# A state-space scan ahead of a SwiGLU layer: chunks of 64 tokens on two row tiles, y in four PSUM banks, one list of steps

## The chip, the cores and the metric

The kernel runs on one core of one Trainium2 chip. The metric is the device time of one execution in microseconds. The kernel before the change takes 417.41 us (median of three runs, 417.39 to 417.42); its profiled execution spans 414.9 us.

## What is computed

Two parts follow one another. The first is a Mamba-2 scan for 4 batches x 8 heads, 768 tokens, head size D = 32 and state size N = 16, all float32. The reference does it in chunks; the length of a chunk changes the amount of work, not the mathematical result:

```python
for c in range(nc):                                   # chunks of a sequence
    cum = np.cumsum(log_a[:, :, sl], axis=-1)
    L = np.exp(cum[..., :, None] - cum[..., None, :]) * causal
    y_intra = (einsum('bhin,bhjn->bhij', Cc, Bc) * L) @ xc
    y_inter = einsum('bhin,bhnd->bhid', Cc, state) * exp(cum)[..., None]
    y[:, :, sl] = y_intra + y_inter
    state = exp(sum(la)) * state + sum_j(Bc_j x_j exp(cum_last - cum_j))
```

The second part takes the 3072 x 256 result y, divides each token by its root mean square, multiplies by a gain, and does a gated layer with d_ff = 1536: `(silu(xn @ w_gate) * (xn @ w_val)) @ w_out`. The output is 3072 x 256, float32.

## The kernel before

Tokens are handled in six blocks of 512; a block has two pairs p of row tiles (128 tokens each), so there are twelve pairs. Block b's feed-forward products stand beside the scan of block b + 1. The gate, value and output products of all but part of the first block use a seven-product scheme on 2 x 2 blocks (`P`, `C`, `O` steps), with the sums done on VectorE.

A chunk is 128 tokens, that is one row tile. TensorE's array is used in tiles in the scan: `tile_position=(row, column)` says where a small matmul lies in the 128 x 128 array. The products C B^T for a pair (step `g`, four row tiles of 32 rows, one for each two heads):

```python
def product(p, todo):
    T = st[p]["T"]
    for i in range(2):
        for q, g in todo:
            r = slice(32 * q, 32 * q + 32)
            nc.tensor.matmul(out=g[:, 256 * i:256 * i + 256], lhsT=T[r, i, 0],
                             rhs=T[r, i, 1:3].rearrange("p t m -> p (t m)"),
                             start=(i == 0), stop=True, tile_position=(32 * q, 0), ...)
```

In the first two pairs this is called for two row tiles at a time (`products`), in the others for all four at once. VectorE then multiplies the products with the decays L, a tile of 128 x (2 x 8 x 128) (`decayed`, `decayed_one`). What a chunk adds to the state (step `A`) and the states (step `S`):

```python
for i in range(n):
    for q in range(NQ):
        nc.tensor.matmul(out=A_ps[32 * q:32 * q + 32, i], lhsT=s["Bd"][:, i, 2 * q:2 * q + 2],
                         rhs=s["x"][:, i, 2 * q:2 * q + 2], tile_position=(0, 32 * q), ...)
# states: one multiplication by a mask for the pair, then for each chunk
nc.vector.scalar_tensor_tensor(out=S, in0=state[g - 1], scalar=fcol[:, k:k + 1],
                               in1=new[:, i], op0=ALU.mult, op1=ALU.add)
```

The output of a pair (step `y`) goes to one pair of PSUM banks; `inter` uses the state, `intra` the chunk's own tokens:

```python
def inter(i, opens):                       # 32 x 64 tiles
    for q in range(NQ):
        nc.tensor.matmul(out=y[o:o + 64, q // 2, i * P:(i + 1) * P], lhsT=S[r],
                         rhs=CdT[r], tile_position=(32 * q, o), ...)
def intra(i, opens):                       # 128 x 32 tiles
    for h in range(NH):
        nc.tensor.matmul(out=y[o:o + 32, h // 4, i * P:(i + 1) * P], lhsT=s["x"][:, i, h],
                         rhs=Ls[p][:, i, h], tile_position=(0, o), ...)
if not first:
    inter(0, True)
intra(0, first)
intra(1, False)
inter(1, False)
```

ScalarE squares y (step `sq`) and copies it out (step `yt`, by VectorE in block 0), one instruction each. The decays of the first four pairs come by matmul: a mask of -2^100 (`mask`, two bf16 matmuls of 512 columns a half of the heads), then sums of logarithms (`sums`, eight matmuls of 128 columns and two of 512), then an exponential. Those of the other pairs are broadcast by DMA from a table of row sums in DRAM (`spread`), VectorE subtracts the token's sum (`sub`), ScalarE takes the exponential and GpSimd clears the part above the diagonal (`ex`).

PSUM has eight banks: three pairs (0, 1 and 2) in the first block, of which 0 and 1 later become four banks for the feed-forward products, and two single banks (`bank`), which serve all small results in turn, among them the two other banks of `g`.

The order of all instructions is written by hand, as a list of steps for each kind of block; each engine executes its own steps in the list's order.

Of the kernel before, what the change touches and what calls it, by code (L numbers as in the profile page):

```python
# [20 lines left out]
def kernel(  # L21
# [47 lines left out]
    NBLK = T // TB  # L69

# [61 lines left out]
    fetched = []  # L132

    def fetch(k=1):
        for _ in range(min(k, len(pieces))):
            n, c, w = pieces.pop(0)
            if n == "o":
                src, dst, shape = wsrc[n][:, c:c + w], wo[:, c:c + w], (w, DM)
            else:
# [8 lines left out]
            fetched.append((w16[:, :, :, 3], (w32[:, :, :, 0], w32[:, :, :, 1]), dst,  # L148
                            [P] + list(shape)))
# [33 lines left out]
    def weight(k):  # L183
        words16, (lo, hi), dst, shape = fetched[k]
        e, f = parts.pop((k, "e")), parts.pop((k, "f"))
        nc.vector.scalar_tensor_tensor(out=dst, in0=f, scalar=2.0 ** -20, in1=e,
                                       op0=ALU.mult, op1=ALU.mult)
        fetch()
# [3 lines left out]
    a_sb = const.tile([BH, S], FP32, name="a_sb")  # L192
# [4 lines left out]
    for p in range(2):  # L197
        load_x(p)
    fetch(2)
    gcol = const.tile([P, 2], FP32, name="gcol")  # L200
    nc.sync.dma_start(out=gcol, in_=moe_rms_g.rearrange("(t p) -> p t", p=P))
    fetch(4)
    load(2)
    load_x(2)
    fetch(3)
    load(3)
    load_x(3)
# [16 lines left out]
                            fill=0.0, base=-1, channel_multiplier=1)  # L224
    hmask = const.tile([P, NH], FP32, name="hmask")
# [21 lines left out]
    nc.vector.tensor_scalar_add(mid[0:64], mid[0:64], -1.0)  # L247
    ident16 = const.tile([P, P], BF16, name="ident16")
    nc.vector.tensor_copy(out=ident16, in_=ident)
    never16 = const.tile([P, P], BF16, name="never16")  # L250
    nc.vector.tensor_copy(out=never16, in_=never)
# [22 lines left out]
    early = nrm.tile([P, 3, NC, BH], FP32, tag="xn", name="early", bufs=1)  # L274
    la0, full, fsel = early[:, 0], early[:, 1], early[:, 2]
# [59 lines left out]
    fcol = const.tile([P, NC * NB], FP32, name="fcol")  # L335

    def chunk_sums():
        ps["c"] = full_ps = bank("full_ps", (P, NC, BH))
        nc.tensor.matmul(out=full_ps.rearrange("p c h -> p (c h)"), lhsT=ones, rhs=laf,
                         start=True, stop=True)  # L340

    def chunk_decays():
        nc.scalar.activation(out=full, in_=ps.pop("c"), func=AF.Exp)
        nc.gpsimd.tensor_tensor(
            out=fsel.rearrange("p c (b h) -> p (c b) h", h=NH),
            in0=full.rearrange("p c (b h) -> p (c b) h", h=NH),
            in1=hmask.unsqueeze(1).to_broadcast([P, NC * NB, NH]), op=ALU.mult)

    def chunk_column():
        nc.vector.reduce_sum(out=fcol, in_=fsel.rearrange("p c (b h) -> p (c b) h", h=NH),  # L350
                             axis=AX.X)


    Ls = {}

    def pair_tile(g):
        if g // 2 not in Ls:
            Ls[g // 2] = ssd.tile([P, 2, NH, P], FP32, tag="L", name="L", bufs=2)
        return Ls[g // 2][:, g % 2]

    def mask(e):
        for i in range(2):
            nc.tensor.matmul(out=e[:, i], lhsT=ident16,  # L363
                             rhs=never16.unsqueeze(1).to_broadcast([P, 4, P]),
                             start=True, stop=False, skip_group_check=True)

    def sums(todo):

        for p, half, e in todo:
            rows_of = [slice(32 * q, 32 * q + 32) for q in (2 * (p % 2), 2 * (p % 2) + 1)]  # L370
            row = rows[p // 2]
            for o in range(4):
                for i, r in enumerate(rows_of):
                    nc.tensor.matmul(out=e[:, i, o * P:(o + 1) * P],  # L374
                                     lhsT=sel[r, 4 * half + o:4 * half + o + 1].to_broadcast([32, P]),
                                     rhs=row[r, 0], start=False, stop=False,
                                     tile_position=(r.start, 0), skip_group_check=True)
            for i, r in enumerate(rows_of):
                nc.tensor.matmul(out=e[:, i], lhsT=row[r, 1],
                                 rhs=sel[r, 4 * half:4 * half + 4].unsqueeze(2).to_broadcast([32, 4, P]),  # L380
                                 start=False, stop=True, tile_position=(r.start, 0),
                                 skip_group_check=True)

    def decay(p, half, e):
        pair_tile(2 * p)
        nc.scalar.activation(
            out=Ls[p][:, :, 4 * half:4 * half + 4].rearrange("p i h m -> p i (h m)"),
            in_=e, func=AF.Exp)

    def spread(g):  # L390
        b, c = divmod(g, NC)
        o = (c * BH + b * NH) * P
        nc.sync.dma_start(out=pair_tile(g).rearrange("p h m -> p (h m)"),
                          in_=rowv[o:o + NH * P].partition_broadcast(P))

    def subtract(g):
# [3 lines left out]
            out=L, in0=L, in1=tok[:, c, b * NH:(b + 1) * NH].unsqueeze(2).to_broadcast([P, NH, P]),  # L400
            op=ALU.subtract)

    def exponential(g):
        L = pair_tile(g)
        nc.scalar.activation(out=L, in_=L, func=AF.Exp)
        nc.gpsimd.affine_select(out=L, in_=L, pattern=[[0, NH], [1, P]], compare_op=ALU.is_ge,
                                fill=0.0, base=0, channel_multiplier=-1)
# [50 lines left out]
    def products(p, half, g):  # L458

        ps["g", p, half] = g  # L460
        product(p, [(2 * half + k, g[:, k]) for k in range(2)])

    def product(p, todo):
        T = st[p]["T"]
        for i in range(2):
            for q, g in todo:
                r = slice(32 * q, 32 * q + 32)
                nc.tensor.matmul(  # L468
                    out=g[:, 256 * i:256 * i + 256], lhsT=T[r, i, 0],
                    rhs=T[r, i, 1:3].rearrange("p t m -> p (t m)"),  # L470
                    start=(i == 0), stop=True, tile_position=(32 * q, 0),
                    skip_group_check=True)

    def decayed(p, half):
# [3 lines left out]
        nc.vector.tensor_tensor(out=L, in0=g.rearrange("p q (i m) -> p q i m", i=2), in1=L,  # L478
                                op=ALU.mult)

    def products_at_once(p, g=None):

# [668 lines left out]
```

## Time and profile before

The profile counts busy time of each engine: TensorE's matmuls (PE), its weight loads (PEld, beside the matmuls), VectorE (DVE), ScalarE (ACT), GpSimd (POOL).

| what | value |
|---|---|
| time, median of three | 417.41 us |
| span of the profiled execution | 414.9 us |
| VectorE, busy | 304.4 us, 667 instructions |
| ScalarE, busy | 229.7 us, 462 instructions |
| data moved by DMA | 27.99 MB, 67 GB/s over the span |
| granted clock of TensorE | full throughout |

The page's chain that ended last is followed back from the last instruction, each step to what released it. Its shares by line tell where the time of the bounding engine goes: 28% and 21% are the gate and value products of line 732 and 23% the output products of line 822, while the scan's lines 468 (g), 550 and 541 (y) and 501 (A) have 4, 3, 2 and 1%. A line such as `L468 PE MATMUL g<-T 32*128 32x256 f32 x192` reads: line, engine, operation, result and operands, the weights' tile in the array, the moving operand's partitions x elements, number of records. Behind it stand the busy time, the mean of one in ns, and the engine's idle time before it. Since matmuls are pipelined, one record's duration is longer than the distance to the next.

### The profile page before, as it was taken

How to read it: one execution, taken by the hardware profiler on the slowest of the kernel's cores; microseconds unless marked ns; L12 is line 12 of the kernel's file. 1: busy time of each engine (PE TensorE's matmuls, PEld its weight loads, DVE VectorE, ACT ScalarE, POOL GpSimd, SP SyncE). 2: the span in 40 equal slices, each digit the busy share in tenths (PEclk: the TensorE clock that was granted, in tenths of full speed). 3: DMA queues.
4: the chain of work that ended last, by engine and by line, in shares of the span. 5: the costliest groups of instructions: out<-in, count | busy, mean ns of one | idle time of the engine just before them, and what ended most of it. 6: DMA issues, size and time to landing. Idle time of an engine off the chain costs nothing.

```text
span 414.9 us, 7936 instructions
## 1 busy us (share of the span) xinstructions
PE 409.7 (99%) x3100; PEld 343.6 (83%) x3100; DVE 304.4 (73%) x667; ACT 229.7 (55%) x462; POOL 39.0 (9%) x48
## 2 busy tenths in 40 slices
PE   7999999999999999999999999999999999999997
PEld 4575478888878799888899887899988889988897
DVE  6899998979679986376986477795575784556672
ACT  3998989877656316745428645526646521245410
POOL 3020000013000005000013100014100000000000
PEclk9999999999999999999999999999999999999999
DMA  9988849001007112703070503070100000100001
GB/s 113 232 200 157 256 102 368 21 0 52 1 2 152 44 61 42 112 2 101 11 145 25 77 2 101 2 154 1 52 2 0 2 2 1 52 0 2 0 2 51
DMA packets 86852, 27.99 MB, mean 67 GB/s; under 512 B 76032, under 2 KB 80640, under 8 KB 86816
## 3 DMA queue, kind: packets, MB, share of 16 engines
q1 hardware_dynamic: 82656, 27.24, 28.3%
q10 hardware_dynamic: 4160, 0.26, 0.8%
q8 instruction: 24, 0.39, 0.4%
q14 instruction: 12, 0.10, 0.1%
HBM read 24.22 MB, written 3.28 MB: 66 GB/s over the span
## 4 chain that ended last, share of the span: by engine, by line
PE 98%; DVE 1%; issue 0%; ACT 0%
PE gate L732 28%; PE o L822 23%; PE val L732 21%; PE o L764 5%; PE g L468 4%; PE gate L648 3%; PE y L550 3%; PE y L541 2%; PE tp L434 2%; PE gate L658 2%; PE A_ps L501 1%; PE e L363 1%; PE rb L613 1%; PE idle L266 1%; PE ms L591 1%; PE e L374 1%
## 5 line engine op out<-in xcount | busy, mean ns | idle before, releaser
L744 DVE TENSOR_TENSOR c<-val,p 128x512 f32<-128x512 f32 x99 | 67.4, 686 | 49.8 <-PE val L732 37.5
L738 ACT COPY p<-gate 128x512 f32<-128x512 f32 x99 | 57.8, 588 | 68.1 <-PE gate L732 62.6
L732 PE MATMUL gate<-tx,sw 128*128 128x256 f32 x264 | 65.0, 382 | 0.0
L732 PEld LDWEIGHTS gate<-tx,sw 128*128 128x128 f32 x264 | 48.7, 190 | 8.2 <-issue 2.0
L757 DVE TENSOR_TENSOR h<-c 128x256 f32<-128x256 f32 x99 | 41.0, 432 | 19.0 <-ACT c L753 19.0
L753 ACT ACTIVATE c<-c 128x256 f32<-128x256 f32 x99 | 38.2, 413 | 11.5 <-DVE c L744 10.7
L732 PE MATMUL val<-xn,sw 128*128 128x256 f32 x132 | 34.1, 383 | 0.0
L732 PE MATMUL val<-tx,sw 128*128 128x256 f32 x132 | 33.8, 384 | 0.0
L822 PE MATMUL o<-wo,h 128*128 128x128 f32 x240 | 33.7, 277 | 0.0
L732 PE MATMUL gate<-tx,wgv 128*128 128x256 f32 x132 | 33.1, 381 | 0.0
L732 PE MATMUL val<-xn,wgv 128*128 128x256 f32 x132 | 33.1, 379 | 0.0
L732 PE MATMUL gate<-xn,wgv 128*128 128x256 f32 x132 | 33.0, 380 | 0.0
L822 PE MATMUL o<-two,s 128*128 128x128 f32 x240 | 32.0, 275 | 0.0
L569 POOL TENSOR_TENSOR sq<-sq 128x256 f32<-128x256 f32 x12 | 10.1, 841 | 227.3 <-ACT sq L568 197.2
L822 PE MATMUL o<-two,h 128*128 128x128 f32 x240 | 30.9, 275 | 0.0
L822 PEld LDWEIGHTS o<-wo,h 128*128 128x128 f32 x240 | 29.9, 192 | 1.0 <-issue 0.6
L822 PEld LDWEIGHTS o<-two,s 128*128 128x128 f32 x240 | 29.9, 192 | 0.3
L838 ACT COPY v<-o 128x256 f32<-128x256 f32 x15 | 5.6, 372 | 43.6 <-PE o L822 43.6
L822 PEld LDWEIGHTS o<-two,h 128*128 128x128 f32 x240 | 28.9, 192 | 0.1
L732 PEld LDWEIGHTS val<-tx,sw 128*128 128x128 f32 x132 | 24.5, 190 | 4.6 <-DVE h L757 1.0
L732 PEld LDWEIGHTS val<-xn,sw 128*128 128x128 f32 x132 | 24.4, 190 | 4.2 <-issue 0.7
L732 PEld LDWEIGHTS gate<-tx,wgv 128*128 128x128 f32 x132 | 24.8, 190 | 3.5 <-issue 0.2
(159 smaller groups left out, 696.9 us busy)
## 6 DMA issues: line engine op xcount, KB each, us to landing
L<-rowd SPq DMA_DIRECT2D x16, 512.0 KB, 4.7
xr<-in_x_dram SPq DMA_DIRECT2D x24, 128.0 KB, 3.5
wr<-in_moe_w_out_dram SPq DMA_DIRECT2D x6, 512.0 KB, 7.2
wr<-in_moe_w_gate_dram SPq DMA_DIRECT2D x5, 512.0 KB, 6.3
wr<-in_moe_w_val_dram SPq DMA_DIRECT2D x5, 512.0 KB, 6.6
out_dram<-ob SPq DMA_DIRECT2D x9, 256.0 KB, 2.2
br<-in_B_dram SPq DMA_DIRECT2D x22, 64.0 KB, 4.2
cr<-in_C_dram SPq DMA_DIRECT2D x22, 64.0 KB, 3.0
```

What stands on the lines that cost most here:

```text
L434: nc.tensor.transpose(out=tp[:, k], in_=src[:, i].rearrange("p h n -> p (h n)"), identity=ident)
L468: nc.tensor.matmul(out=g[:, 256 * i:256 * i + 256], lhsT=T[r, i, 0], rhs=T[r, i, 1:3].rearrange("p t m -> p (t m)"), start=(i == 0), stop= ...
L550: nc.tensor.matmul(out=y[o:o + 32, h // 4, i * P:(i + 1) * P], lhsT=s["x"][:, i, h], rhs=Ls[p][:, i, h], start=opens, stop=True, tile_posi ...
L569: nc.gpsimd.tensor_tensor(out=sqs[blk][:, tk], in0=sq2[:, 0], in1=sq2[:, 1], op=ALU.add)
L648: nc.tensor.matmul(out=gv[:, k], lhsT=w[:, t, fs], rhs=xns[0][:, t], start=(t == 0), stop=(t == 1))
L732: nc.tensor.matmul(out=dst[:, half[w]], lhsT=lhsT, rhs=rhs, start=(k in (1, 2, 5) and w == 0), stop=True, skip_group_check=True)
L738: nc.scalar.copy(out=t, in_=Xs[j])
L744: nc.vector.tensor_tensor(out=t, in0=Zs[j], in1=a, op=ALU.add)
L753: nc.scalar.activation(out=u, in_=src[:, half[0]], func=AF.Silu)
L757: nc.vector.tensor_tensor(out=hidden_tile(blk, j)[:, c // 10 - 1, c % 10 - 1], in0=u, in1=src[:, half[1]], op=ALU.mult)
L764: nc.tensor.matmul(out=o, lhsT=hs_[blk, f // 2][:, f % 2, k // 2, (k % 2) * P:(k % 2 + 1) * P], rhs=wo[:, f], start=opens, stop=(f == NF - ...
L822: nc.tensor.matmul(out=o[t] if apart else o[:, t * P:(t + 1) * P], lhsT=lhsT[:, t], rhs=rhs, start=(k in (1, 2, 4, 5) and j == 0 and (apar ...
```

## The change

A chunk is now 64 tokens, half a row tile. Two chunks of the same row tile are handled at once: the second index u in `halves` picks tokens 0 to 63 or 64 to 127, which lie on the upper or lower half of the array's rows (in `A` and intra y) or go to the lower or upper half of its columns (in `g`). The decays L within a chunk have a quarter of the elements of a 128-token chunk, and there are twice as many chunks, so L is half as large. In return there are twice as many states. Matmuls are shorter and there are more of them, in up to eight tiles at a time. Different row tiles write to different PSUM banks: `A` takes both single banks, y the pair 2 and both single banks, four in all. All steps of all blocks stand in one list with the block's number ahead of each step, in a new order in which steps of neighbouring blocks mix; the list also says which pair of banks each step of the first block takes, and when each piece of the weights is fetched.

The core of the diff (cuts marked by [...]; setup of masks and constants, the table of row sums in DRAM and the list itself left out):

```diff
+    HC = P // 2
+    halves = [slice(0, HC), slice(HC, P)]
[...]
-            Ls[g // 2] = ssd.tile([P, 2, NH, P], FP32, tag="L", name="L", bufs=2)
+            Ls[g // 2] = ssd.tile([P, 2, NH, HC], FP32, tag="L", name="L", bufs=LBUFS)   # LBUFS = 4
[...]
+    def sums(p, e):                     # once a pair, was: once for each half of the heads
+        for h in range(NH):
             for i, r in enumerate(rows_of):
+                for u in halves:
+                    nc.tensor.matmul(out=e[u, i, h * HC:(h + 1) * HC],
+                                     lhsT=sel[r, h:h + 1].to_broadcast([32, HC]), rhs=row[r, 0, u],
+                                     tile_position=(r.start, u.start), ...)
+        for i, r in enumerate(rows_of):
+            for u in halves:
+                nc.tensor.matmul(out=e[u, i], lhsT=row[r, 1, u], rhs=sel[r]...([32, NH, HC]),
+                                 tile_position=(r.start, u.start), ...)
[...]
     def product(p, todo):
         for i in range(2):
             for q, g in todo:
                 r = slice(32 * q, 32 * q + 32)
-                nc.tensor.matmul(out=g[:, 256 * i:256 * i + 256], lhsT=T[r, i, 0],
-                    rhs=T[r, i, 1:3]..., tile_position=(32 * q, 0), ...)
+                for u in halves:
+                    nc.tensor.matmul(out=g[u, P * i:P * i + P]..., lhsT=T[r, i, 0, u],
+                        rhs=T[r, i, 1:3, u], tile_position=(32 * q, u.start), ...)
[...]
     def additions(p):
-        ps["A", p] = A_ps = bank("A_ps", (P, 2, 2, D))
+        ps["A", p] = A_ps = [bank("A_ps", (P, 2, 2, D)) for u in range(2)]
+        for i, u in chunks_of(p)[2]:        # four chunks; three in the last pair of a sequence
             for q in range(NQ):
-                    lhsT=s["Bd"][:, i, ...], rhs=s["x"][:, i, ...], tile_position=(0, 32 * q), ...
+                    lhsT=s["Bd"][halves[u], i, ...], rhs=s["x"][halves[u], i, ...],
+                    tile_position=(HC * u, 32 * q), ...
[...]
     def outputs(p, y):
+        y = [y[:, 0], y[:, 1], bank("y2", (P, 512)), bank("y3", (P, 512))]
-        inter(0), intra(0), intra(1), inter(1)
+        for i in range(2):                  # inter, all chunks (not the first of a sequence)
+            for u in range(2):
+                for q in range(NQ):
+                    product_y(q // 2, u, i, slice(o, o + 64), lhsT=S[r],
+                              rhs=s["T"][r, i, 3, halves[u]], tile_position=(32 * q, o))
+        for i in range(2):                  # intra
             for h in range(NH):
+                for u in range(2):
+                    product_y(h // 4, u, i, slice(o, o + 32), lhsT=s["x"][halves[u], i, h],
+                              rhs=Ls[p][halves[u], i, h], tile_position=(HC * u, o))
[...]
+    def parts_of_y(p):                  # squares and taken_out run once for each part
+        y = ps["y", p]
+        return [(0, slice(0, 2), ps["y pair", p][:, :, 0:P])] + [
+            (1, slice(u, u + 1), y[2 + u][:, 0:P].unsqueeze(1)) for u in range(2)]
[...]
-    for blk in range(1, NBLK):
-        order = """ P.1.0 take.1.0 ... """       # one list for each kind of block
+    order = """ 0:fetch.16 0:r.0 ... 5:quarter.0.1.1 """
```

Two places of the new list, with a block's number ahead of the colon. Block 0 ends among block 1's products: `1:P.6.0 1:P.7.1 1:C.11.1 1:take.6.0 1:P.5.1 1:P.7.0 0:wt.19 1:take.7.0 1:two.4 0:o.10 0:o.11`. A scan's end: `2:A.1 2:s3.0 2:L.1 2:take.6.4 2:P.7.4 2:take.7.4 2:hid.11.3 2:s.3 2:C.22.5 2:P.3.5 2:silu.22.5 2:s3.3 2:S.1 2:y.1 2:sq.1`. Instructions in the two kernels as built:

| group | before | after |
|---|---|---|
| g, matmuls | 96 of 256 columns | 192 of 128 |
| y from L, matmuls | 192 of 128 | 384 of 64 |
| y from the state, matmuls | 80 of 128 | 176 of 64 |
| A, matmuls | 80 | 176 |
| masks / row sums | 16 / 64 + 16 | 8 / 128 + 16 |
| state updates on VectorE | 16 | 40 |
| masks of A on VectorE | 12 | 24 |
| squares of y / copies by ScalarE | 12 / 10 | 36 / 30 |
| table loads on ScalarE | 18 | 13 |

## The prediction

> **What bounds the kernel now.** I read the page first, its busy shares and the chain that ended last:
>
> ```profile
> PE 409.7 (99%) x3100; PEld 343.6 (83%) x3100; DVE 304.4 (73%) x667; ACT 229.7 (55%) x462; POOL 39.0 (9%) x48
> PE 98%; DVE 1%; issue 0%; ACT 0%
> ```
>
> TensorE is busy 409.7 of 414.9 us and 98% of the last chain runs on it: matmul time is the kernel's time, and idle time elsewhere costs nothing as long as TensorE finds work. Whether that holds everywhere I took from a table of stretches (length, then busy time of PE, PEld, DVE, ACT, POOL, then clock, DMA):
>
> ```profile
> 0.00:22.50 22.50, 19.99 (x243) 12.28 (x243) 17.06 (x55) 15.11 (x32) 3.98 (x15) 1.00 1.08 172
> 22.50:101.00 78.50, 78.50 (x494) 57.06 (x491) 73.33 (x144) 69.23 (x115) 9.62 (x9) 1.00 0.53 143
> 165.00:229.30 64.30, 64.30 (x514) 56.29 (x513) 46.01 (x99) 34.02 (x71) 6.69 (x7) 1.00 0.33 65
> 357.00:415.00 58.00, 55.21 (x338) 50.61 (x336) 31.86 (x76) 19.45 (x45) 0.00 (x0) 1.00 0.04 14
> ```
>
> Two things are to be seen. A middle block (third row) keeps TensorE full while VectorE needs 46.0 of 64.3 us: room there. From 22.5 to 101 us VectorE is at 73.3 of 78.5 us, a close second. The last block has no scan of a next block beside it and takes 58 us, some 6 us less than a middle one: that is what two pairs of scan cost.
>
> Which matmuls does the change touch? Groups of TensorE with shapes kept apart (a busy time is the union of modelled times, a matmul in f32 has two records):
>
> ```profile
> L468 PE MATMUL g<-T 32*128 32x256 f32 x192 | 16.8, 402 | 0.0
> L550 PE MATMUL y<-L,xr 128*32 128x128 f32 x384 | 12.9, 275 | 0.0
> L541 PE MATMUL y<-T,S 32*64 32x128 f32 x160 | 9.0, 293 | 0.0
> L363 PE MATMUL e<-never,ident 128*128 128x512 bf16 x16 | 4.8, 382 | 0.0
> L501 PE MATMUL A_ps<-xr,Bd 128*32 128x64 f32 x160 | 4.7, 226 | 0.0
> ```
>
> The modelled ends overlap the next start, so for the true cost of a burst I used the timeline and took the start of a burst to the start of what follows (start, length, group):
>
> ```profile
> 17.27 0.43 PE L501 MATMUL A_ps<-xr,Bd 128*32 128x64 f32 x16
> 17.63 1.13 PE L468 MATMUL g<-T 32*128 32x256 f32 x8
> 18.69 1.08 PE L550 MATMUL y<-L,xr 128*32 128x128 f32 x32
> 19.70 0.45 PE L541 MATMUL y<-T,S 32*64 32x128 f32 x8
> ...
> 39.50 1.15 PE L468 MATMUL g<-T 32*128 32x256 f32 x16
> 40.58 3.70 PE L648 MATMUL gate<-xn,wgv 128*128 128x512 f32 x8
> ...
> 47.97 0.32 PE L501 MATMUL A_ps<-xr,Bd 128*32 128x64 f32 x8
> 48.22 1.12 PE L648 MATMUL gate<-xn,wgv 128*128 128x512 f32 x2
> ```
>
> So A takes 17.63 - 17.27 = 0.36 us for 16 records and 48.22 - 47.97 = 0.25 us for 8: 0.11 us per 8 records plus 0.14 us to fill and drain. The 8 are two waves of four column tiles, so a wave with 64 columns takes 0.055 us. Intra y (32 records, eight waves, 128 columns) takes 1.01 us = 8 x 0.109 + 0.14. g takes 1.06 us for 8 records and 1.08 us for 16: with four row tiles at once instead of two, **twice the work costs the same time**. That pair of lines is the case for the whole change. Four waves of 256 columns make 0.86 of it, so its fixed part is 0.21. Inter y takes 0.38 us (the burst in its other places in the timeline) = 2 x 0.107 + 0.17.
>
> [...]
>
> **Part by part, on TensorE.** A wave is taken at 0.055 us for 64 columns and 0.109 for 128, as above, however many tiles are in it.
> - g: 16 matmuls of 128 columns a pair of row tiles of tokens, on 4 x 2 tiles: 32 records, four waves: 4 x 0.109 + 0.2 = 0.64 us. Before: ten pairs x 1.08 and the first two pairs in halves, 4 x 1.06, plus what was interleaved and stalled, 15.5 us in all from start to start. After 12 x 0.64 = 7.7. **Saves 7.8.**
> - y: intra is 32 matmuls of 64 columns on eight tiles: 64 records, eight waves, 8 x 0.055 + 0.15 = 0.6 us against 1.01. Inter is up to 32 records in eight waves of four, 0.6 us, in one burst against two of 0.38 (one in the four pairs that open a sequence). Before 12 x 1.01 + 20 x 0.38 = 19.7; after 8 x 1.2 + 4 x 1.1 = 14.0, rounded up to 14.4 for the turn from one form to the other. **Saves 5.2.**
> - A: twice the matmuls, eight tiles, the same waves: 0.36 as before; the four pairs that end a sequence had half a burst (0.25) and now have 0.34. **Costs 0.4.**
> - The decays of the first four pairs, by matmul: half the masks (16 of 512 columns become 8), 4.4 us to 2.1. The row sums: a half took 0.54 us (0.23 + 0.31), two a pair; now 32 short ones in 8 waves of four and four wide ones at once, some 0.55 a pair. **Saves 2.3 and 2.3.**
> - Two chunk sums instead of one: costs 0.3.
> Sum: 7.8 + 5.2 - 0.4 + 4.6 - 0.3 = **16.9 us** off TensorE. The feed-forward matmuls are the same in number and form.
>
> **The other engines.** VectorE: 16 subtractions (1215 ns) and 14 wide multiplications (1218) halve to the price of a 512-column one (about 680): -16.1; 20 narrower ones go from 682 to some 425: -5.1; 24 more state updates at 285 and 12 more masks of A at 284: +10.2; setup +0.6. In sum -10, off the path in a middle block. ScalarE: each squaring and each copy of y becomes three (596 to 372 + 2 x 278 = 928 ns), +7.5; the exponentials halve, -12; five table loads fewer at 1283, -6.4: about -11. GpSimd keeps its work, in twice the instructions; the broadcasts by DMA halve. None of this sets the end, but two things now press on TensorE: y holds both single banks as well as the pair until six ScalarE instructions (some 1.9 us) are through, and all four state updates must be ready before intra y starts, where before intra ran ahead of the second inter.
>
> **The rivals.**
> 1. *Eight tiles are bound by issue.* If a record costs A's 14 ns whatever the tiles, intra y is 64 x 0.014 + 0.14 = 1.02 us, no gain, and A 0.58: 12 x 0.64 = 7.7 us are lost again, about 410 us. For it: eight tiles are new here. Against it: within A's bursts the 14 ns are explained by data (four tiles in 0.055 us).
> 2. *VectorE becomes the bound of the first 101 us.* It had 90.4 us of work there and loses only about 2.5 (six wide multiplications, four narrow, four subtractions, less the added states), while TensorE loses some 10 and would want about 91. For it: 88 of 91 us can't be packed without waits. Against it: the one list now lets the last weights, combined weights and a subtraction of block 0 sit among block 1's products, where VectorE had 13 us of room. It would give back 3 to 6 us.
> 3. *The head stays a chain.* In the first 22.5 us TensorE loses about 6 us of work but sums, exponentials, products and states follow one another. Perhaps half of it is not seen: 3 us.
> 4. *Waits for banks or states around y*, 0.5 us in half of the twelve pairs: 3 us. If the list is badly matched to the new times, far more, up to the whole gain.
>
> **Range and chances.** 417.4 - 16.9 = 400.5 would be the case without any new wait. I choose to give back 2 for the head and 1 for waits around y and the first stretch, less than the rivals' sum since the new list was evidently laid out for the shorter bursts: 403. Low 396.5 is the full gain and a few microseconds of old gaps closed by the order; high 410 is rival 1 or rivals 2 to 4 together. Faster by over 2% needs less than 409.1 us: 0.83. Within 2%: 0.14. Slower by over 2% would need a plain failure of the order: 0.03.
>
> **What would show it.** In the changed profile g should take 0.64 us to the next burst, inter y 0.6, intra y 0.6 (1.0 means rival 1), the five groups together 17 us less. A middle block should last about 62.5 us with TensorE still full. TensorE's idle time should be within 6 us of the span; a gap before y with the state or a ScalarE copy as releaser is rival 4, and gaps before 101 us released by VectorE are rival 2 or 3. I am wrong if TensorE's share falls below about 96%, or if records in the eight-tile bursts lie 14 ns apart.

## The result, and the profile after

The changed kernel takes **422.86 us** (median of four runs, 422.62 to 423.76) against 417.42 us of the kernel before on the same chip: a ratio of 1.0138, 95% interval 1.0124 to 1.0152. It is 1.4% slower where 403 us were predicted. The profiled executions span 420.9 and 414.9 us.

First the page of the changed kernel: busy shares, the granted clock in 40 slices of the span, and the chain that ended last.

```profile
PE 407.2 (97%) x4118; PEld 344.6 (82%) x4118; DVE 301.7 (72%) x712; ACT 216.4 (51%) x497; POOL 43.5 (10%) x64
PEclk9988999999999999999999999999999999999999
PE 81%; DVE 9%; ACT 3%; DMA 3%; SPq 2%; issue 1%; DVEq 0%; ACTq 0%
```

TensorE's share of the chain fell from 98 to 81%: VectorE, ScalarE, transfers and SyncE's queue now stand on it. TensorE is idle for 420.9 - 407.2 = 13.7 us, before 5.2, and its clock is below full in the first slices.

The groups of the touched matmuls, shapes kept apart (busy us, mean ns | idle before them):

```profile
L555 PE MATMUL y<-L,xr 64*32 64x64 f32 x768 | 11.0, 235 | 1.4 <-issue 1.4
L555 PE MATMUL y<-T,S 32*64 32x64 f32 x352 | 9.1, 231 | 1.5 <-DVE A L528 0.9 <-DVE yt L607 0.6
L475 PE MATMUL g<-T 32*64 32x128 f32 x384 | 8.9, 287 | 0.0
L515 PE MATMUL A_ps<-xr,Bd 64*32 64x64 f32 x352 | 5.8, 223 | 1.0 <-DVE A L528 0.8 <-ACT T L467 0.2
```

g halved (16.8 to 8.9 us). The two parts of y hardly moved (12.9 + 9.0 to 11.0 + 9.1), and y and A have idle time in front of them, which they had not. The timeline shows single bursts, as it did in the prediction (start, length, group, idle time before it); the first two lines are the last burst of y ahead of the feed-forward work, with a stop of 1.38 us inside, which is taken up below:

```profile
31.52 0.45 PE L555 MATMUL y<-L,xr 64*32 64x64 f32 x30
33.34 0.80 PE L555 MATMUL y<-L,xr 64*32 64x64 f32 x34 [1.38 <-issue]
...
178.67 0.69 PE L475 MATMUL g<-T 32*64 32x128 f32 x32
179.30 1.13 PE L758 MATMUL val<-xn,wgv 128*128 128x256 f32 x4
...
210.39 0.69 PE L555 MATMUL y<-T,S 32*64 32x64 f32 x32
211.01 0.86 PE L555 MATMUL y<-L,xr 64*32 64x64 f32 x64
211.80 1.13 PE L758 MATMUL gate<-tx,wgv 128*128 128x256 f32 x4
```

From start to start g takes 179.30 - 178.67 = 0.63 us, inter y 0.62 and intra y 0.79. The first feed-forward matmul starts at 34.06 us, before at 22.47; these are the first eight of them, before and after:

```profile
22.47 1.99 PE L658 MATMUL gate<-yt,wgv 128*128 128x256 f32 x8
34.06 3.25 PE L684 MATMUL gate<-yt,wgv 128*128 128x256 f32 x8
```

Where the time went is read by cutting both traces where the same amount of feed-forward work is done:

| feed-forward work done | before, at | after, at | behind by |
|---|---|---|---|
| none | 22.5 us | 34.1 us | 11.6 |
| 24 us of it | 59.8 | 66.0 | 6.2 |
| 59.4 us (end of the first block's products) | 98.5 | 106.2 | 7.7 |
| then four blocks, one after the other | 163.6, 228.0, 292.4, 357.0 | 171.2, 234.8, 299.0, 362.1 | 7.6, 6.8, 6.6, 5.1 |
| all | 414.9 | 420.9 | 6.0 |

So the loss is made ahead of 35 us. By the second row 5.4 us of it are back, since the new order has the decays of pairs 2 and 3 ahead of the first feed-forward matmul; the 1.5 us lost in the third are a g and an A that the old order had earlier (1.1 us) and a wait for VectorE (0.4). The four blocks win 2.6 back, and the last stretch, which has no scan beside it, loses 0.9 (58.8 us, before 57.9). The ends of the four blocks hold to about 0.4 us only, since the two kernels have the feed-forward matmuls in a different order. The table of stretches has it too (length, then busy time of PE, PEld, DVE, ACT, POOL, clock, DMA):

```profile
0.00:34.10 34.10, 25.11 (x509) 16.27 (x509) 23.63 (x82) 18.58 (x40) 4.35 (x15) 0.94 1.01 182
34.10:106.20 72.10, 71.60 (x592) 53.52 (x592) 64.80 (x136) 55.38 (x108) 7.87 (x10) 0.98 0.54 127
171.20:234.80 63.60, 63.60 (x679) 56.23 (x678) 42.78 (x101) 31.35 (x77) 6.03 (x8) 1.00 0.20 35
...
26.40:29.80 3.40, 3.40 (x125) 2.28 (x126) 3.23 (x10) 2.48 (x7) 0.73 (x1) 0.50 1.05 399
```

In the first 34.1 us TensorE is idle for 9.0 (before: 2.5 of 22.5), and no other engine is full either: VectorE 23.6, ScalarE 18.6 of 34.1. That is a chain of waits, not a new bound. In the middle block (third row, before 64.3 us) TensorE is as full as it was. The last row is one of the steps of 3.4 us in which the record of the clock grants one half; the other one between here and full clock is 33.2 to 36.6 us. What sets the clock to one half there no trace shows.

What did the engines wait for? The waits of 4 to 36 us:

```profile
ACT e L169 <- DMA wr<-in_moe_w_gate_dram: 3.9, 1, 3.9
DVE Cd L430 <- DMA cr<-in_C_dram: 3.5, 1, 3.5
DVE m L179 <- DMA wr<-in_moe_w_gate_dram: 2.5, 1, 2.5
PE r_ps L312 <- ACT la L291: 2.0, 1, 2.0
```

The first and third: ScalarE's and VectorE's conversion of the first weights (`pow.0`, `man.0`) stand in the new list ahead of the first pair's exponential, and the weights land at 13.5 us; the exponential of pair 0 runs at 15.04 instead of 8.69 us (the lines below, before and after). The second: the scaling of pair 3's C (`scale.3`) stands ahead of VectorE's copy of y, and its C lands at 35.9 us. The fourth: seven more instructions that build constants stand on VectorE ahead of the clip of a, so the logarithms start at 6.2 instead of 4.8 us.

```profile
8.69 1.02 ACT L386 ACTIVATE L<-e 128x1024 f32<-128x1024 f32 x1 [2.12 <-PE e L379]
15.04 1.00 ACT L397 ACTIVATE L<-e 128x1024 f32<-128x1024 f32 x1
```

### The profile page after: what moved, and what is told of

Its sections match the earlier page's. It is cut to its first block, busy times and chain, and to the rows that moved or that the text cites. A ratio compares the mean times of both kernels' runs of the same rounds, so it can differ in the third digit from the quotient of the medians.

```text
span 420.9 us, 10070 instructions
## 1 busy us (share of the span) xinstructions
PE 407.2 (97%) x4118; PEld 344.6 (82%) x4118; DVE 301.7 (72%) x712; ACT 216.4 (51%) x497; POOL 43.5 (10%) x64
## 4 chain that ended last, share of the span: by engine, by line
PE 81%; DVE 9%; ACT 3%; DMA 3%; SPq 2%; issue 1%; DVEq 0%; ACTq 0%
PE gate L758 25%; PE o L848 21%; PE val L758 19%; PE o L790 4%; PE y L555 3%; PE gate L674 3%; PE tp L445 1%; PE g L475 1%; SPq L115 1%; DMA br<-in_B_dram 1%; SPq L109 1%; DMA wr<-in_moe_w_gate_dram 1%; DVE c L770 1%; DMA cr<-in_C_dram 1%; DVE h L783 1%
## 5 line engine op out<-in xcount | busy, mean ns | idle before, releaser
L758 PE MATMUL gate<-tx,sw 128*128 128x256 f32 x264 | 66.6, 383 | 0.9 <-DVE sw L728 0.6
L779 ACT ACTIVATE c<-c 128x256 f32<-128x256 f32 x99 | 40.3, 419 | 31.9 <-DVE c L770 31.4
L758 PE MATMUL val<-tx,sw 128*128 128x256 f32 x132 | 34.1, 382 | 0.4 <-DVE c L770 0.4
L758 PE MATMUL gate<-xn,wgv 128*128 128x256 f32 x132 | 34.2, 384 | 0.0
L594 POOL TENSOR_TENSOR sq<-sq 128x256 f32<-128x256 f32 x12 | 8.8, 734 | 208.8 <-ACT sq L591 161.2
L848 PE MATMUL o<-wo,h 128*128 128x128 f32 x240 | 30.3, 276 | 0.0
L848 PE MATMUL o<-two,s 128*128 128x128 f32 x240 | 29.2, 277 | 0.1
L848 PE MATMUL o<-two,h 128*128 128x128 f32 x240 | 28.9, 275 | 0.0
L848 PEld LDWEIGHTS o<-two,s 128*128 128x128 f32 x240 | 27.9, 192 | 0.9 <-DVE s L821 0.3
L417 POOL TENSOR_SCALAR_AFFINE_SELECT L<-L 64x512 f32<-64x512 f32 x32 | 22.1, 692 | 59.4 <-ACT L L415 40.1
L758 PEld LDWEIGHTS val<-xn,wgv 128*128 128x128 f32 x132 | 24.8, 190 | 3.6 <-issue 0.2
```

The lines of the kernel that those rows point to most:

```text
L417: nc.gpsimd.affine_select(out=L[r], in_=L[r], pattern=[[0, NH], [1, HC]], compare_op=ALU.is_ge, fill=0.0, base=0, channel_multiplier=-1)
L594: nc.gpsimd.tensor_tensor(out=sqs[blk][:, tk], in0=s2[:, 0], in1=s2[:, 1], op=ALU.add)
L758: nc.tensor.matmul(out=dst[:, half[w]], lhsT=lhsT, rhs=rhs, start=(k in (1, 2, 5) and w == 0), stop=True, skip_group_check=True)
L779: nc.scalar.activation(out=u, in_=src[:, half[0]], func=AF.Silu)
L848: nc.tensor.matmul(out=o[t] if apart else o[:, t * P:(t + 1) * P], lhsT=lhsT[:, t], rhs=rhs, start=(k in (1, 2, 4, 5) and j == 0 and (apar ...
```

## Experiments

Times are medians; ratios are to the kernel before on the same chip, with a 95% interval. All but e8, e12 and e15 start from the changed kernel. `step.p` are names of the list.

**One cause at a time.** Three possible ones were undone each alone: the half speed of the start (two mask matmuls take 1.06 us at 16.96, 0.59 at 21.70), the constants, and the weights' conversions; then the scaling of pair 3.

e1_warm, twelve throw-away matmuls behind the first transposes, to keep the clock up:

```diff
+    for k in range(12):
+        nc.tensor.matmul(out=idle[:, 0, 0:256], lhsT=warm[:, 0:P], rhs=warm, ...)
```

> The changed kernel with twelve more throw-away bf16 matmuls behind the transposes of a, where TensorE now idles for 2 us. Theory A (the half clock of the head, [...]costs time by itself): full clock from about 6 us instead of 19.6, and 2 to 4 us less, 419 to 421. Theory B (engines that work in order stand behind weight conversions whose DMA has not landed): the exponential still ends near 16 us, less than 1 us gained, 422 to 423. Theory C (chunks of 64 tokens cost the time): no change.

Measured: 423.08 us, 1.0141 (1.0113 to 1.0170). First feed-forward matmul at 34.6 us. No gain. The clock did not stay up, though: it was full by 9 us, and the record grants half from 12.4 to 22.6 and from 29.5 to 39.7 us again, and TensorE stands still for 2.8 us from 11.6 us on, waiting for VectorE.

e2_setup, the new constants on VectorE behind the clip of a:

> The changed kernel with the VectorE constants that nothing needs before the logarithms moved behind the clip of a: the clip starts near 4.4 us instead of 5.84. If the start of the chain decided (theory D), 1.5 us less, 421.4. Under theory B the exponential waits for the first weight piece at 13.5 us either way: less than 0.5 us gained[...].

Measured: 422.26 us, 1.0118 (1.0096 to 1.0139); first feed-forward matmul at 34.4 us.

e3_conv, the conversions of the first pieces moved back in the list, `scale`, `sums` and `exp` ahead of them:

```diff
- 0:cx 0:pow.0 0:turn.0.1 ... 0:Tt.0.0.1 0:man.0 0:Tt.0.0.0 ... 0:exp.0 0:man.1
+ 0:cx 0:turn.0.1 ... 0:exp.0 0:d 0:dx ... 0:yt.0 0:ydone.0 0:pow.1 ... 2:load.0 0:man.0
```

> The changed kernel with the conversions of the first four weight pieces moved back behind the exponentials and products of the first two pairs (as the kernel before had them); nothing else. Theory B: the first exponential at about 12.3 instead of 15 us, no wait of ScalarE and VectorE for the weights, and 4 to 7 us less, 416 to 419. Theory A alone: at most 1 us. Theory C: no change.

Measured: 422.23 us, 1.0123 (1.0101 to 1.0145); first feed-forward matmul at 33.2 us.

e5_scale, only `scale.3` later:

```diff
- 0:sq.1 0:scale.3 0:fetch.10 ... 0:rowout.0 0:man.8
+ 0:sq.1 0:fetch.10 ... 0:rowout.0 0:scale.3 0:man.8
```

> The changed kernel with one step moved: the scaling of pair 3 (VectorE, reads C and B of pair 3, whose DMA can only start when pair 0 is done) stands behind the norm's roots instead of ahead of the copies of pair 1. Theory E (VectorE waits in order for that DMA until about 35 us and holds the copies of pair 1, and with them the banks that TensorE needs next): VectorE's 3.5 us wait at 32 us goes, 3 to 5 us less, 418 to 420. If the early part decides (theories A, B, D), no change.

Measured: 422.85 us, 1.0142 (1.0124 to 1.0161). The 3.5 us of VectorE for C are gone and 1.9 us for a square of ScalarE stand in their place.

None alone is worth more than about 0.8 us by its ratio, and each interval overlaps that of the changed kernel.

**The same together.** e4_all3 has the first three at once, e6_scale_conv the conversions and the scaling, e7_scale_all3 all four.

> The three edits together. Theories A, B and D add up to 7 to 11 us: first feed-forward matmul near 24 us, 412 to 416, faster than the kernel before. If theory C holds, it stays above 418.

> The same with the weight conversions moved back as well. Alone they gave 0.6 us. Theory E: the late DMA hid what they win, so now the two add to 6 to 9 us, 414 to 417. If the conversions never mattered: as the scaling alone.

> The same with the setup and the twelve throw-away matmuls as well: all four edits. Theory E with A, B and D: the first feed-forward matmul near 29 us and no gap behind it, 410 to 414, faster than the kernel before. Theory C (chunks of 64 tokens cost the time): above 418.

Measured: e4 423.38 us, 1.0154 (1.0138 to 1.0169); e6 420.90, 1.0096 (1.0081 to 1.0111); e7 420.50, 1.0091 (1.0064 to 1.0119). In e4 the first feed-forward matmul is 5.2 us earlier (28.9), but TensorE then waits 4.0 us for VectorE's copy of y, which stands behind the scaling. With the scaling moved too, about 2 us are left as a gain (by the ratios 1.8 in e6 and 2.0 in e7). The waits lie one behind another: removing the first uncovers the next.

**Is one misplaced step enough in the old kernel?** e8_before_scale: the kernel before, with nothing but `scale.3` moved forward to where the new list has it, behind the first early products.

```diff
- yt.0 wt.1 sq.1 ydone.0 early.0.0 man.2 rowout.1 ... silu.0 scale.3 norm.1
+ yt.0 wt.1 sq.1 ydone.0 early.0.0 scale.3 man.2 rowout.1 ... silu.0 norm.1
```

> The kernel before (chunks of 128, its own list) with that one step moved the other way: the scaling of pair 3 to just behind the first early product, ahead of the copies of pair 1. Theory E: VectorE waits there for the DMA of C, 2 to 5 us more, 419 to 422, with none of the rest of the change. If the harm comes from the short chunks: no change.

Measured: 429.47 us, 1.0292 (1.0275 to 1.0309). Its waits from 20 to 45 us:

```profile
DVE Cd L419 <- DMA cr<-in_C_dram: 10.6, 1, 10.6
...
PE ms L591 <- DVE r_sb L911: 10.0, 1, 10.0
```

One step of two VectorE instructions of 0.42 us each, whose data come late, stands ahead of others in VectorE's order and costs 12.5 us, with TensorE waiting behind it. This is shown for the old operations; the same line costs the new kernel less, whose VectorE gets there later and waits 3.5 us, not 10.6.

**Is it the half speed of the start?** e12_before_cold: the kernel before with one throw-away matmul at the start instead of twelve.

> The kernel before with one throw-away matmul at the start instead of twelve, nothing else. Theory A (an idle TensorE brings the half clock, and that costs time in the head): half clock for at least the first 7 us and 1 to 4 us more, 418 to 421. If the head is bound by other engines, within 0.5 us.

Measured: 416.98 us, 0.9994 (0.9985 to 1.0002). Its timeline has the matmuls at about half speed at first and at full speed from 10.2 us, while the table of stretches gives the clock as 1.00 from 0 on:

```profile
6.62 1.06 PE L363 MATMUL e<-never,ident 128*128 128x512 bf16 x2
...
11.38 0.60 PE L363 MATMUL e<-never,ident 128*128 128x512 bf16 x2
```

The same two matmuls take 1.06 us at 6.62 and 0.60 at 11.38 (0.59 at 6.04 in the kernel before, behind its twelve throw-away matmuls), and the median does not move. In the trace, which is that of the slowest of the twelve executions, the first feed-forward product comes at 23.21 instead of 22.47 us, so up to 0.7 us can hang on it there. In the old kernel, then, a start at half speed costs no more than the noise. For the changed kernel this is not settled: in e1 the clock fell again. Half the clock later, under the first feed-forward products (0.50 granted from 33.2 to 36.6 us), is another matter: the first eight early products last 3.25 us in the changed kernel, 1.99 in the old.

**The head rewritten.** e9_head2 orders the first 40 us as the old kernel did: conversions behind the scan, squares and copies of y ahead of conversions, scaling late. e10_head2_all adds the constants and the warm-up, e11_head2_intra puts intra y ahead of inter y as well, so that y need not wait for the states at first.

> The changed kernel with the list of its first 40 us put in the kernel before's manner: conversions behind the scan of the first two pairs and in the order in which the pieces land (0 and 1 first), no conversion ahead of the states, squares and copies of y ahead of conversions, the scaling of pair 3 late, block 0's first early product before its second. Theory F (several steps of the new list stand ahead of their data, each hiding the next; all must go): first feed-forward matmul near 26 us, 413 to 417. Theory C (short chunks cost the time) or A alone: 420 or more.

> The same with the setup moved behind the clip and twelve throw-away matmuls in the gap before the first sums. Theory F with A and D: another 2 to 3 us, 410 to 414, faster than the kernel before by 1%.

> The same again with intra y ahead of inter y in all pairs, so that a pair's own states have 0.8 us more until TensorE reads them. If the wait for the four state updates costs time outside the head, 1 to 2 us less than without; if not, within 0.5 us.

Measured: e9 423.49 us, 1.0138 (1.0092 to 1.0185); e10 **419.99, 1.0068 (1.0053 to 1.0083)**, the best version of the changed kernel; e11 420.85, 1.0085 (1.0070 to 1.0100). In e10 the first feed-forward matmul starts at 27.6 us, 24 us of the work are done at 63.9 us, and from there to the end it takes 355.0 us, the old kernel 355.1. What is left is 4 us in the head. The 3 us between e9 and e10 come from the constants and the warm-up together; no run separates them. e11 gains nothing over e10, so the wait for the states outside the head is not worth the 1 to 2 us that were thought possible. TensorE's waits in the head of e10 are of a new kind, without a releaser: two of 0.81 and 0.55 us within y, one of 0.71 within A, and the longest ahead of the transposes of B:

```profile
8.93 0.30 PE L447 MATMUL tp<-ident,br 128*128 128x128 f32 x1 [1.87 <-issue]
```

One like this last is in e7, e11, e13, e14, e17 and e18 too (1.73 to 1.88 us). It costs little in e10, since the sums that come next need a row that VectorE has ready at 9.67 us only; its cause is open.

**Stops without a releaser.** Two kernels whose TensorE streams differ in nothing but twelve throw-away matmuls ahead of them tell more about those within y and A (the constants that e10 also moves are on VectorE). e9, without them:

```profile
22.94 0.63 PE L555 MATMUL y<-L,xr 64*32 64x64 f32 x36
24.16 0.45 PE L555 MATMUL y<-L,xr 64*32 64x64 f32 x28 [0.59 <-issue]
```

e10, with them:

```profile
20.69 0.43 PE L557 MATMUL y<-L,xr 64*32 64x64 f32 x24
21.93 0.89 PE L557 MATMUL y<-L,xr 64*32 64x64 f32 x40 [0.81 <-issue]
```

In the same burst the stop comes after 36 records without and after 24 with the twelve: it moved by exactly the twelve. Counted from the start, weight loads and matmuls each as one, it is before the 694th record in both. The stop in the next burst (in the changed kernel itself between the 30 and the 34 records shown above) is before the 950th, 256 later, with or without the twelve; one before the 439th, 255 ahead of the 694th, is in e4, e6, e7, e10 and e16: in A, but in e6 in the row sums, so it does not belong to one kind of matmul. The profile pages have a line for the queue that brings instructions (packets, MB, share), before and after:

```profile
q8 instruction: 24, 0.39, 0.4%
q8 instruction: 32, 0.52, 0.5%
```

A packet has 16,384 bytes. The changed kernel has 8 packets more and, weight loads and matmuls together, 8236 - 6200 = 2036 records of TensorE more, 254 a packet. Each of the stops at 694 and 950 ends 2.2 to 3.0 us after such a packet began. The stops are 255 and 256 records apart, so my reading of these counts is that **the supply of instructions stops TensorE**, where the scan's short records use them up fastest; no run switched the stops on or off at will. (The expectation of e16 below says that all ten runs have both stops. That is too much: 694 was seen in e1, e2, e9, e10, e11, e14 and e18, 950 in the changed kernel and in e1, e2, e3, e5, e9, e10, e13 and e14; in the others another wait lies there or none was seen.)

Can it be avoided? e13_fetch_late fetches the weights behind the inputs of the third pair, e16_head3 moves the decays of pairs 2 and 3 behind the first feed-forward products, e17_head3_early also puts those products between the two bursts of y, and e15_before_small adds 96 tiny matmuls to each of the first two bursts of the old kernel.

```diff
 e13: - fetch(2, 3, 4, 5) ... fetch(6, 7, 8) ... 0:fetch.16
      + 0:rowout.1 0:fetch.2.3.4.5.6.7.8.16
 e16: - 0:mask.2/2 0:Tl.0 0:A.0 ... 0:sums.2 ... 0:exp.2 0:mask.3/0 0:sq.0 0:sums.3
      + 0:early.0.0/1 0:mask.2/0 0:sums.2 0:exp.2 ... 0:mask.3/0 0:sums.3
 e17: + 0:scale.2 0:early.0.0/1 0:y.1/2
 e15: + for k in range(96):
      +     nc.tensor.matmul(out=y[0:32, 0, 0:32], lhsT=warm[:, 0:32], rhs=warm[:, 0:32], ...)
```

> The last rewrite of the head (head list in the old manner, constants behind the clip, warm-up), with the weight pieces 2 to 8 and 16 fetched behind the third pair's inputs and the row sums instead of ahead of them. Theory: TensorE's unexplained stops in the head (1.87, 0.71, 0.81 and 0.55 us, all without a releaser) come from instruction fetches that stand behind the weights in full DMA queues. With the weights later the last three shrink below 0.3 us each, [...]and the kernel gains 2 to 5 us: 415 to 418. Rival: the stops come from the number of small instructions alone, whatever else is on the queues: the same stops, 420 +- 1, or worse, if conversions now wait for their weights.

Measured: 421.64 us, 1.0108 (1.0088 to 1.0128). The stop before the 950th record is 1.07 us, not shorter. The weights on the queues are not its cause; the rival holds, and the conversions start later.

> The kernel before the change, with 96 throw-away bf16 matmuls of 32 columns ahead of y in each of the first two pairs (they write where y is opened afterwards). 192 records at some 14 to 25 ns are 2.7 to 4.8 us of TensorE time themselves. Theory of supply: TensorE also shows stops without a releaser in or behind these bursts, 0.5 us or more each, as in the changed kernel's head, and the kernel takes over 421. Rival: no such stops, the bursts cost their own time, 420 to 422 us, with the granted clock full throughout.

Measured: 422.17 us, 1.0122 (1.0107 to 1.0137), no stop. The 96 records take 2.4 us, 25 ns each, on one tile of the array. With their weight loads these are 192 records in 2.4 us, so 256 would take 3.2 us (an estimate), longer than the 2.2 to 3.0 us from the beginning of a packet to the end of a stop: probably too slow to outrun the supply, so this run could not show it. It cost its own time.

> The rewrite of the head as before (old manner, constants behind the clip, warm-up), and the decays of pairs 2 and 3 by matmul (masks, sums, exponentials) moved from ahead of and between the first two bursts of y to behind the first feed-forward products, where the old kernel has them. In all ten runs of the changed kernel's operations the stops without a releaser end before the same records of TensorE's stream, weight loads and matmuls counted: the 694th and the 950th, 256 apart, 2.3 to 2.9 us after a 16-KB instruction fetch began. Theory of supply: the move takes 152 instructions from in front of y.1, so the 950th falls behind it; a stop, if any, stands again before about record 694 (or 439) of the new stream, which is now in y.1, and the 950th has none. TensorE is idle less, the kernel gains 1 to 3 us: 417 to 419. Rival: the stops belong to the y bursts themselves (their banks, their operands): they stay in the same place of y.0 and y.1, other indices, 420 +- 1.

> The same, and the first two feed-forward tiles' early products (eight records of 256 columns, 1.73 us) stand between the bursts y.0 and y.1 instead of behind them. Theory of supply: feed-forward records use up instructions ten times slower than a burst of y, so the fetch catches up in between: no stop without a releaser in y.1 of over 0.3 us, and another 0.5 to 1 us gained over the run beside it, unless the products then wait for their weights' conversion on VectorE. Rival: no change beyond 0.3 us, or worse: TensorE in order waits for the converted weights (over 1 us with VectorE as releaser) and y.1 behind it is late.

Measured: e16 422.23 us, 1.0114 (1.0094 to 1.0134); e17 423.11, 1.0130 (1.0103 to 1.0158). The waits of e16, then of e17, from 17 us:

```profile
PE ms L628 <- ACT mr L625: 2.3, 1, 2.3
PE A_ps L517 <- issue: 0.9, 1, 0.9
```

```profile
PE ms L628 <- ACT mr L625: 3.1, 1, 3.1
```

In e16 the stop is again before the 439th record, now the 24th of A instead of the 22nd, because two matmuls ahead of it are gone. Neither run has a stop in y of the first two pairs, as the theory said; but y ran at half the clock in both (granted from 20.3 to 30.6 us in e16, 18.6 to 28.8 in e17), so the missing stop proves less. And both kernels are slower than e10: the exponentials now stand on ScalarE ahead of the norm, and TensorE waits for that. The time was not won by taking the stops away.

**The slow half of y.** Intra y takes 0.79 us where 0.6 was predicted: in all undisturbed bursts its records, eight at a time, start 80, 56, 56, 76, and from the 32nd on 147, 67, 67, 94 ns on. The 147 hold a pause of some 85 ns at the 32nd record itself. e14_split_y puts feed-forward matmuls between the first and the second 32 records in four blocks. In two places the moved matmuls add a product to a bank before a sum is read that should be without it, so the output differs; the instructions are the same in number and form. e18_alternate lets the records alternate between the two row tiles.

```diff
 e14: - inter(all); intra(0); intra(1); P
      + inter(all); intra(0); P; intra(1)
 e18: - for i in range(2):          + for h in range(NH):
      -     for h in range(NH):     +     for i in range(2):
```

> The same rewrite of the head, and in blocks 1 to 4 the burst y is cut in two: inter y and the intra records of the first row tile, then four (in two places six) feed-forward matmuls, then the intra records of the second row tile. Theory: the last 31 or so records of an uncut burst lie 10 ns apart instead of 6.7 because the supply of instructions runs dry in a deep burst. Then the second part, standing alone after feed-forward matmuls, takes 0.22 us plus 0.14 to fill and drain, 0.36, where it took 0.47, and what is gained is lost again at the two more switches: within 1 us of 420. Rival: the later records are slow for what they write (the second half of each bank) and stay 10 ns apart: the second part takes 0.47 us or more, and the kernel 421 to 422.

> The rewrite of the head, and in intra y the loop over the two row tiles moved inside the loop over the heads: the 64 records alternate between the two row tiles instead of taking 32 of the first and then 32 of the second. In the changed kernel the first 24 records start 55 to 80 ns per eight, then 76, 147, 67, 67, 94: the slowing begins at the 32nd record of intra whether 0, 24 or 32 records of inter y stand ahead of it. Theory of supply: [...]the same pattern, slow from the 32nd record, 0.79 us in all, 420 +- 1. Rival: the pause belongs to the change from the first row tile to the second (other columns of the banks, other operands): it goes or is spread evenly over all records; if it goes, intra takes 0.6 us and the kernel gains some 2 us: 418.

Measured: e14 427.49 us, 1.0241 (1.0205 to 1.0277). The burst at 211 us, cut in two:

```profile
211.50 0.46 PE L561 MATMUL y<-L,xr 64*32 64x64 f32 x32
211.89 1.13 PE L772 MATMUL gate<-tx,wgv 128*128 128x256 f32 x4
212.95 0.46 PE L561 MATMUL y<-L,xr 64*32 64x64 f32 x32
213.34 1.13 PE L772 MATMUL val<-xn,sw 128*128 128x256 f32 x4
```

Standing alone, the second half takes 213.34 - 212.95 = 0.39 us, like the first; within the burst it took 0.52. It is not slow for what it writes. (The total does not show this: in the trace, which is that of the fastest of four executions, TensorE waits 2.3 us more than in e10 between feed-forward matmuls, 1.8 of them for VectorE in one block, and loses 2.1 more in changes from one form to the other. The rest of the 7.5 us between the two medians is not explained.) e18 takes 421.60 us, 1.0113 (1.0094 to 1.0133):

```profile
208.88 1.01 PE L557 MATMUL y<-L,xr 64*32 64x64 f32 x64
209.82 1.13 PE L760 MATMUL gate<-tx,wgv 128*128 128x256 f32 x4
```

Intra is 0.94 us, and the slowing again begins at the 32nd record, 198 ns for those eight, although what changes there is no longer the row tile but the pair of banks, a change that the usual order has at its 16th record without slowing. It begins there whether 0 (e11), 24 or 32 records of inter y go before. What the 32nd record runs into no trace shows; that alternating made it worse says that what follows depends on the order of the operands, and why was not tried.

## Why the prediction was wrong

- **The bursts: g, A and the decays right, y too low.** g 0.63 us (predicted 0.64), A 0.38 (0.36), inter y 0.62 (0.6). Rival 1 fell: the first records of intra y are 7 ns apart, not 14. The decays by matmul take 4.4 us in e10 against 9.0 in the old kernel, the 4.6 predicted. The term that was mis-sized is intra y: eight waves of 0.055 us hold for four of them only; 0.79 us, so y is 1.41 and 1.30 where 1.2 and 1.1 were predicted. Eight pairs of the one and four of the other are 16.5 us instead of 14.4. The sum of 16.9 us becomes 14.8.
- **The step that failed is the last one:** "I choose to give back 2 for the head and 1 for waits around y and the first stretch ... since the new list was evidently laid out for the shorter bursts." With 14.8 us less work and 6.0 us more span, 20.8 us were given back. Measured from each record's start to the next, up to 98.5 us before and 106.2 us after, TensorE's time went thus (so a wait stands with the record ahead of it; the 0.8 us in which A waits for VectorE are in the row of the decays):

| TensorE, up to the end of the first block's products | before | after |
|---|---|---|
| g | 6.8 us | 3.4 |
| decays by matmul | 9.0 | 6.8 |
| y, with what it waits for | 6.3 | 10.3 |
| A | 1.3 | 2.2 |
| logarithms, sums and first transposes, with what they wait for | 6.1 | 12.9 |
| between feed-forward matmuls, and half clock | 1.8 | 3.3 |

 The first four rows should have shrunk by 9 us together (g 4.3, decays 4.6, y 0.9, less the small additions); they shrank by 0.7 (23.4 to 22.7), since y took on waits, and the last two grew by 8.3, most of it the logarithms, sums and transposes. With the 7.7 us of delay, 17 of the 20.8 us lie here.
- **Rivals 3 and 4 were the right ones and were put at 3 us each.** The head stayed a chain and the list put four steps ahead of their data. But even in the best order tried they don't explain all: undoing them, with the constants and the warm-up, gains 3 us (e10). At the end of the first block's products e10 is still 5.7 us behind (104.2 against 98.5, the changed kernel 7.7), so it undoes about 2 of the 17 us. The traces show where the rest is lost, but no run removed it. The stops without a releaser (0.55 to 0.81 us within y and A) and a granted clock of 0.50 from 21.4 to 31.6 us are among them, and how much is the chain, how much the stops and how much the clock is open: each attempt to remove one wait brought forward another (e13, e16, e17).
- **Rival 2, VectorE as the bound up to 101 us, is small:** from 34 to 107 us TensorE waits 0.4 us for it, and VectorE is busy for 64.8 of 72.1 us. VectorE's waits ahead of 34 us belong to the chain of the head.
- **The blocks gain less than predicted.** They take 65.0, 63.6, 64.2 and 63.1 us, before 65.1, 64.4, 64.4 and 64.6, where 62.5 was predicted. In these blocks and the last together g wins 3.8 us and y 2.3; A costs 0.6, a wait for VectorE's sums of weights behind the transposes 0.6, and gaps between feed-forward matmuls, with the changes from one form to the other, 2.8 (0.3 of it a wait for ScalarE). No run tried the old order in the blocks with the short chunks; that it would win more is not shown.
- TensorE's share, 97%, stayed over the 96 below which I wanted to call myself wrong, and the idle time of 13.7 us, predicted within 6, showed it. A share of a long span hides a lost head.

## What to carry to other kernels

When a change makes work cheaper and also rewrites the order, price the order by itself: for each engine, ask of every step moved forward when its data land, since one step of under 1 us that waits for a transfer cost 12 us here (e8). Waits that lie one behind another are not worth their sum: undo them together before judging. And halving the size of small matmuls doubles the instructions; look in the densest few microseconds for stops without a releaser, and count at which record of the stream they come, before putting them down to the array.

## What the hardware showed that was not expected

- TensorE stopped for 0.5 to 2.3 us at a fixed place of its instruction stream (records 439, 694 and 950, that is 255 and 256 apart), whatever stood there, in the densest part of the scan. In the old kernel, with 3100 records instead of 4118, no such stop was seen.
- A burst of 64 short records on eight tiles starts them some 7 to 8 ns apart up to the 32nd and then, with a pause there, about 12 on average (0.79 us in all), or 16 when neighbours alternate between row tiles (0.94 us); bursts of 32 don't show it (A 0.38 us, the halves of intra y in e14 0.39).
- Matmuls at about half speed for the first 10 us (1.06 us for two that take 0.60 later) cost no more than noise in the old kernel's median (e12), while the eight feed-forward products that a step of 3.4 us at a granted clock of 0.50 met took 3.25 us, 1.99 in the old kernel.
